# Fetching the first chunk of x as fp32 from two hardware queues, with the cast on VectorE and ScalarE

## The chip, the cores and the metric

The kernel runs on one core of a Trainium2 chip. A core has a matrix engine (TensorE, PE in the profile; its weight loads are listed apart as PEld), a vector engine (VectorE, DVE), an engine for activations (ScalarE, ACT), a general one (GpSimd, POOL) and one that only issues transfers (SyncE, SP). Sixteen DMA engines carry out the transfers of all queues. In the profile, q0 is the queue that GpSimd fills by software, q1 is SyncE's hardware queue and q10 is ScalarE's. The metric is the device time of one execution in microseconds; smaller is better.

## The reference

```python
def _attn_ref(x, filt_r, filt_i):
    X = np.fft.rfft(x, axis=1)
    F = (filt_r + 1j * filt_i)[None, :, :]
    Y = X * F
    y = np.fft.irfft(Y, n=x.shape[1], axis=1)
...
def _moe_ref(x, w_gate, w_val, w_out, rms_g):
    rms = np.sqrt(np.mean(x * x, axis=-1, keepdims=True) + 1e-06)
    xn = x / rms * rms_g
    g = xn @ w_gate
    silu = g * (1.0 / (1.0 + np.exp(-g)))
    val = xn @ w_val
    return (silu * val @ w_out).astype(np.float32)
```

x has 8 sequences of 3008 rows of 256 fp32 numbers. Each sequence is filtered along its length in the frequency domain, and each of the 24064 resulting rows then goes through a normalisation and a gated feed-forward layer of width 1536.

## The kernel before

The Fourier transforms are matrix products. 3008 is split as 64 times 47: the first step, a product with the 128x128 matrix `wa`, transforms along the 64; the second one, with `wb`, along the 47; the product with the filter and the way back (`wi`, `wai`) follow. Then every block of 512 rows is normalised and goes through the feed-forward products (lines 546 and 563), which fill nearly the whole span. While one sequence is in the feed-forward layer, the transforms of the next ones are fitted between its products by a planner (from line 718 on). Before that stands a prologue of about 44 us, written out by hand in program order, in which sequence 0 is transformed with nothing to overlap it. The change lies at the start of this prologue, and the steps of the prediction are all in it.

Each of the 128 partitions holds 24 rows of a sequence (the last of every other partition is not used), and x is loaded in four chunks of 6 of them (`XC = 6`, `NXC = 4`). `x_load` (line 174) takes a tile of pool `xp` in fp16 and has GpSimd's queue load and cast it in one transfer, since x lies in memory as fp32; GpSimd's queue is the one that casts. In the prologue GpSimd issues, in this order: the four chunks of sequence 0 (lines 614 and 615), the blocks of the filter `fs` (`f_load`, line 382), the tables `wb` and `wi`, and the weights. At most eight of its transfers are in flight: the ninth waits until the first has landed. SyncE issues the table `tab`, which holds `wa`, `wai` and the identity matrices (line 616), and three small loads of the last filter row and the norm's gain into `tail`.

TensorE starts with `fill(10)`: ten products of zeros with zeros (line 426) that compute nothing. `a0_unit` (line 353) then does the first step for four rows of each partition: four products of 128x128 with a slice of x as the stationary operand and `wa`, a part of `tab`, as the moving one (line 357), and a copy of the result (`psa`) to `uu`. `a0(g)` does both halves of group g, with ScalarE copying the one and VectorE the other (`copy`, line 193, whose own lines 195 and 197 stand in the profile). Group 0 needs rows 0 to 3 and group 1 rows 4 to 7, so that group 0 needs two thirds of chunk 0, and group 1 the rest of it and the start of chunk 1. The order on TensorE is as follows; between the second and the third row of fills stand five small transposes of `tail` (lines 650 and 651):

```python
        fill(10)
        a0(0)
        fill(4)
        a0(1, 2)
        ...
        fill(3)
        a0(3)
        fill(4)
        a0(4, 5)
```

After that come `f_unit` (line 385), which transposes the filter blocks through TensorE into `psf` (line 389), and `tr0_unit` (line 367), which transposes the result of the first step; then the second step for sequence 0.

The pool `stg` has four buffers. They are used in turn by the filter blocks, the weights before their scaling (`w_load`) and, later, the rows before the norm (`y_tile`).

Of the kernel before, what the change touches and what calls it, by code (L numbers as in the profile page):

```python
# [10 lines left out]
FP32 = mybir.dt.float32  # L11
FP16 = mybir.dt.float16
# [5 lines left out]
N1 = 47  # L18
N2 = 64
NF = N // 2 + 1  # L20
P = 128
D = 256
# [3 lines left out]
H = 24  # L26
# [7 lines left out]
XC = 6  # L34
NXC = H // XC
# [66 lines left out]
def kernel(  # L102
# [11 lines left out]
    nc = tc.nc  # L114
# [9 lines left out]
    stg = ctx.enter_context(tc.tile_pool(name="stg", bufs=4))  # L124
    xp = ctx.enter_context(tc.tile_pool(name="xp", bufs=4))
# [38 lines left out]
    st = {b: {"x": {}, "t1": {}, "t2": {}, "s": {}, "yt": {}, "t4": {}, "y": {}, "sq": {},  # L164
              "u": {}, "xn": {}} for b in range(B)}

    def raw(src, row, ap):
        return bass.AP(tensor=src.tensor, offset=src.offset + row * D, ap=ap)
# [5 lines left out]
    def x_load(b, c):  # L174
        t = xp.tile([P, XC, D], FP16, tag="xc", name="xc")
        row = b * N + c * XC
        src = lambda n, w, lo=0: raw(x.flatten_outer_dims(), row + lo, [[N1 * D, n], [H * D, 2], [1, w * D]])
        if b == B - 1 and c == NXC - 1:
            w = XC - 1
            nc.vector.memset(t[96:P, w, :], 0.0)  # L180
            nc.gpsimd.dma_start(t[:, 0:w, :].rearrange("p a d -> p (a d)"), src(N2, w))
            nc.gpsimd.dma_start(t[0:P - 2, w, :], src(N2 - 1, 1, w))
            nc.gpsimd.dma_start(t[P - 2:P - 1, w, :],
                                raw(x.flatten_outer_dims(), row + w + (N2 - 1) * N1, [[D, 1], [1, D]]))
        else:
            nc.gpsimd.dma_start(t.rearrange("p a d -> p (a d)"), src(N2, XC))  # L186
        st[b]["x"][c] = t

    def bank(i, name):
        pool, tag = ((psM, "mx"), (psG, "pg"), (psV, "pv"), (psB, "mb"), (psO, "po0"))[i]  # L190
        return pool.tile([P, 512], FP32, tag=tag, name=name)

    def copy(eng, out, in_, scale=None):
        if eng == "A":
            nc.scalar.activation(out=out, in_=in_, func=AXT.Copy, **({} if scale is None else {"scale": scale}))  # L195
        elif scale is None:
            nc.vector.tensor_copy(out=out, in_=in_)
        else:
            nc.vector.tensor_scalar(out=out, in0=in_, scalar1=scale, scalar2=None, op0=ALU.mult)
# [223 lines left out]
    def fill(n, bk=0):  # L423
        ps = bank(bk, "pf")
        for _ in range(n):
            nc.tensor.matmul(ps, ss3[0][:, 0, 0, :], ss3[0].rearrange("p k e q -> p (k e q)")[:, 0:512], start=True, stop=True)
# [181 lines left out]
                                        op0=ALU.mult, op1=ALU.mult)  # L608

    with tc.manual_schedule():  # L610
        nc.vector.memset(ss3[0], 0.0)
        nc.vector.memset(epsb, 1e-6 * Y_SCALE * Y_SCALE)
        nc.scalar.activation(out=warm, in_=epsb.to_broadcast([P, 4]), func=AXT.Sqrt)
        for c in range(NXC):
            x_load(0, c)
        nc.sync.dma_start(tab, tab_d)
        tail = op.tile([P, 4, D], FP32, tag="o3", name="tail")
# [20 lines left out]
        def a0(*gqs):  # L638
            for gq in gqs:
                for dh in range(2):  # L640
                    a0_unit(gq, dh, E[dh], 1 + dh)

        fill(10)
        a0(0)
        fill(4)
        a0(1, 2)
# [32 lines left out]
        for p in range(UN + 3):  # L679
            if 3 <= p < UN:  # L680
                b_unit(0, od[p], (0, 3)[p % 2])
                s_part(0, od[p], 1)
            if p == 0:
                f_unit(2, 1, 1, "A")
                f_neg(4, 12, (1,))
                f_last()
                f_neg(0, 4)
                w_load(2)
                wo_load(0)
                f_neg(16, 16)  # L690
                wo_load(1)
                for c in range(3):
                    x_load(1, c)
                for q in range(3):
                    w_gain(q)
            if 2 <= p < UN + 1:
                yt0_unit(od[p - 2], "A", 1)
            if p == UN + 1:
                yt0_unit(UN - 1, "V", 1, slice(0, 2))
                yt0_unit(UN - 1, "A", 0, slice(2, 4))  # L700
            if 4 <= p < UN + 3:
                bi_unit(0, od[p - 4], "AV"[p == UN + 1], 2)
            if UN + 1 <= p < UN + 3:
                fill(1, 1)
# [8 lines left out]
        nc.gpsimd.tensor_copy(out=seen, in_=st[0]["t4"][1][:, 0, 0:4])  # L713
        wo_load(2)
        x_load(1, 3)
        first_norm()

# [92 lines left out]
        for b in range(1, B):  # L810
            t = (b - 1) * 72
# [73 lines left out]
```

## Time and profile before

| | |
|---|---|
| time, median of 3 runs | 863.4 us (863.33 to 864.85) |
| span of the profiled execution | 861.4 us |
| TensorE busy | 852.4 us, 99% of the span |
| ScalarE busy | 612.4 us, 71% |
| VectorE busy | 557.2 us, 65% |
| GpSimd busy | 297.8 us, 35% |
| read from HBM, written to it | 45.78 MB, 35.65 MB |

The profile is that of one execution. Its span begins with the first instruction that was recorded and ends with the last; times within it are counted from its start. A row of the timeline gives the start, the duration from the first to the last of the grouped instructions, the engine, the line, the operation, the tiles (written one, arrow, read ones), their shape and number, and in brackets how long the engine had been idle before and what ended that. SPq is SyncE's queue of issues; the duration of a DMA row there is that of issuing, not of the transfer. A row of the chain that ended last gives start, duration and what the end of the program was waiting on then. A row of a DMA queue gives its packets, the megabytes and the share of the sixteen engines' time in that window.

### The profile page before, as it was taken

Reading aid. Unit: us, or ns where it says so; the run is one execution under the profiler, and the core shown is the slowest. Engines: PE = TensorE matmul, PEld = TensorE weight load, DVE = VectorE, ACT = ScalarE, POOL = GpSimd, SP = SyncE. Lnnn points to the kernel's source line nnn. Section 1 sums busy time; section 2 is a strip of 40 time slices with the busy share of each in tenths; the row PEclk is TensorE's granted clock in tenths of the full one; section 3 lists DMA queues with packets and bytes.
Section 4 is the critical chain, followed back from the end, with each engine's and each line's share of the span. In section 5 each row is a group of like instructions: output and inputs, shape, how many; then the busy total and the mean of one; then the engine's idle time right before and its main releaser. Section 6 shows DMA issues by size and latency. Waiting matters only on the chain.

```text
span 861.4 us, 17024 instructions
## 1 busy us (share of the span) xinstructions
PE 852.4 (99%) x6142; PEld 532.2 (62%) x6142; DVE 557.2 (65%) x926; ACT 612.4 (71%) x1339; POOL 297.8 (35%) x346
## 2 busy tenths in 40 slices
PE   8999999999999999999999999999999999999997
PEld 6755666566666666666666666666666666665664
DVE  5857655776666666666666676767666665555554
ACT  4986777787588756887577856888567765777443
POOL 5725742453144322534034430444123430132000
PEclk9999999999999999999999999999999999999999
DMA  9995778765975476656755548433564331521101
GB/s 283 270 204 124 150 164 168 139 130 121 197 137 129 121 150 111 151 107 147 139 127 113 132 98 180 108 87 101 131 127 93 97 70 42 124 54 49 62 25 50
DMA packets 198237, 107.98 MB, mean 125 GB/s; under 512 B 158566, under 2 KB 182520, under 8 KB 198152
## 3 DMA queue, kind: packets, MB, share of 16 engines
q1 hardware_dynamic: 189464, 85.52, 44.1%
q0 software_dynamic: 8544, 21.24, 12.7%
q8 instruction: 48, 0.79, 0.4%
q14 instruction: 37, 0.30, 0.1%
q10 hardware_dynamic: 144, 0.13, 0.0%
HBM read 45.78 MB, written 35.65 MB: 95 GB/s over the span
## 4 chain that ended last, share of the span: by engine, by line
PE 96%; DMA 1%; ACT 1%; DVE 1%; issue 0%; POOL 0%; POOLq 0%
PE po L563 28%; PE pg L546 28%; PE pv L546 28%; PE psb L241 3%; PE psi L285 3%; PE psn L314 2%; PE psa L206 2%; DMA fs<-in_filt_i_dram 1%; PE psy L418 1%; PE psf L389 1%; PE pst L367 0%; ACT sg L550 0%; POOL xc L186 0%; DVE s L231 0%; DVE hh L551 0%
## 5 line engine op out<-in xcount | busy, mean ns | idle before, releaser
L551 DVE TENSOR_TENSOR hh<-pv,sg 128x512 f16<-128x512 f32 (+2 forms) x578 | 391.5, 678 | 286.4 <-ACT sg L550 221.9
L550 ACT ACTIVATE sg<-pg 128x512 f16<-128x512 f32 (+2 forms) x578 | 337.4, 584 | 217.6 <-PE pg L546 213.4
L546 PE MATMUL pg<-xn,wg 128*128 128x512 f16 (+2 forms) x1156 | 338.1, 374 | 0.1
L546 PE MATMUL pv<-xn,wv 128*128 128x512 f16 (+2 forms) x1156 | 338.1, 374 | 0.0
L563 PE MATMUL po<-wo,hh 128*128 128x256 f16 x2256 | 332.7, 273 | 0.0
L563 PEld LDWEIGHTS <-hh 128*128 128x128 f16 x2256 | 213.4, 98 | 105.5 <-issue 0.6
L268 POOL TENSOR_TENSOR ss<-s,s 128x384 f16<-128x384 f16 x112 | 101.9, 911 | 273.2 <-DVE s L234 245.2
L546 PEld LDWEIGHTS <-wv 128*128 128x128 f16 x1156 | 112.9, 98 | 130.7
L546 PEld LDWEIGHTS <-wg 128*128 128x128 f16 x1156 | 111.4, 98 | 17.0 <-issue 0.3
L340 POOL TENSOR_TENSOR xt<-y,rho 128x1024 f16<-128x1024 f32 (+1 forms) x46 | 85.4, 1856 | 2.8
L322 ACT ACTIVATE junk<-y 128x256 f16<-128x256 f32 x180 | 74.3, 413 | 2.8
L231 DVE TENSOR_TENSOR s<-psb,ff 128x384 f16<-128x384 f32 x124 | 67.6, 547 | 0.7 <-ACT ff L195 0.6
L234 DVE TENSOR_TENSOR s<-psb,ff 128x384 f16<-128x384 f32 x124 | 67.6, 546 | 0.0
L195 ACT ACTIVATE uu<-psi 128x384 f16<-128x384 f32 (+1 forms) x127 | 61.6, 486 | 1.5 <-DMA out_dram<-o 0.5
L195 ACT ACTIVATE y<-psn 128x512 f32<-128x512 f32 (+1 forms) x95 | 55.7, 588 | 4.2
L285 PEld LDWEIGHTS <-yt 96*128 96x128 f16 x512 | 35.4, 97 | 26.7 <-issue 1.0
L332 POOL TENSOR_TENSOR rho<-u,mhalf 128x4 f32<-128x4 f32 (+1 forms) x46 | 46.5, 1010 | 3.8
L330 POOL TENSOR_SCALAR u<-ss 128x4 f32<-128x4 f32 (+1 forms) x46 | 8.9, 193 | 104.8 <-ACT junk L322 103.8
L195 ACT ACTIVATE t<-psa 128x512 f16<-128x512 f32 x70 | 41.4, 594 | 3.1 <-PE psa L206 1.7
L285 PE MATMUL psi<-wi,yt 96*128 96x96 f16 x512 | 42.9, 205 | 0.1
L241 PE MATMUL psb<-wb,t 96*128 96x96 f16 x480 | 40.1, 206 | 0.3 <-DVE s L234 0.2
L241 PEld LDWEIGHTS <-t 96*128 96x128 f16 x480 | 28.7, 97 | 12.8 <-DVE s L234 3.3
(101 smaller groups left out, 366.2 us busy)
## 6 DMA issues: line engine op xcount, KB each, us to landing
out_dram<-o SPq DMA_DIRECT2D x40, 512.0 KB, 3.6
xc<-in_x_dram POOLq DMA_DIRECT2D x31, 384.0 KB, 5.6
z_tmp<-t SPq DMA_DIRECT2D x28, 384.0 KB, 2.7
t<-z_tmp SPq DMA_DIRECT2D x28, 384.0 KB, 6.0
out_dram<-o SPq DMA_DIRECT2D x7, 384.0 KB, 2.7
fs<-in_filt_i_dram POOLq DMA_DIRECT2D x3, 512.0 KB, 10.8
fs<-in_filt_r_dram POOLq DMA_DIRECT2D x3, 512.0 KB, 11.2
ws<-in_moe_w_gate_dram POOLq DMA_DIRECT2D x3, 512.0 KB, 9.8
```

The source lines that it names most:

```text
L195: nc.scalar.activation(out=out, in_=in_, func=AXT.Copy, **({} if scale is None else {"scale": scale}))
L231: eng.tensor_tensor(out=o, in0=ps, in1=f1, op=ALU.mult)
L234: eng.tensor_tensor(out=o, in0=ps[:, :, ::-1, :], in1=f2, op=ALU.mult)
L241: nc.tensor.matmul(ps[:, ts(k, KR)], st[b]["t2"][kk // KC][:, kk % KC, ds(dh * P, P)], wb[0:KR, kk, :], start=True, stop=True)
L268: nc.gpsimd.tensor_tensor(out=ss3[g % 3][:, :, dh, 0:KR], in0=s[0], in1=s[1], op=ALU.add)
L285: nc.tensor.matmul(ps[:, k, :], yt[0:KR, k, dh, :], wi[0:KR, 4 * g + k, :], start=True, stop=True)
L322: nc.scalar.activation(out=junk, in_=y[:, i, ts(u, D)], func=AXT.Square, accum_out=ss[:, 2 * i + u:2 * i + u + 1])
L340: nc.gpsimd.tensor_tensor(out=xt[:, 0:n, :], in0=y.rearrange("p a (u d) -> p (a u) d", u=2)[:, 0:n, :], in1=rho[:, 0:n].unsqueeze(2).to_br ...
L546: nc.tensor.matmul(ps[:, 0:w], wt[:, dt_, ts(jt, P)], xn[:, q0:q1, dt_, :], start=(dt_ == 0), stop=(dt_ == 1))
L550: nc.scalar.activation(out=sg[:, c], in_=pg[:, 0:w], func=AXT.Silu)
L551: nc.vector.tensor_tensor(out=hh[:, c], in0=pv[:, 0:w], in1=sg[:, c], op=ALU.mult)
L563: nc.tensor.matmul(po[s4 // 2][:, s4 % 2, :], hh[:, ts(s4, P)], wo[:, jt, :], start=(jt == 0 and s4 % 2 == 0), stop=(jt == JT - 1 and (s4 ...
```

## The change

The first chunk of sequence 0 is no longer loaded by GpSimd. A new function `x_first` takes its fp16 tile as before and a staging buffer in fp32 from `stg`, and issues two transfers without a cast: SyncE loads the first four rows of each partition (`X0 = 4`), ScalarE the other two. It is called ahead of everything else, so that these are the first instructions of the two engines: `tab` and the three small loads come behind SyncE's part, and the load of ScalarE's function table comes behind ScalarE's part. GpSimd begins with chunk 1. On TensorE the first row of fills is cut from ten to seven. After it in program order VectorE casts the first four rows to fp16 and ScalarE the other two, ahead of their copies of `psa`.

```diff
+    X0 = 4
+
+    def x_first():
+        t = xp.tile([P, XC, D], FP16, tag="xc", name="xc")
+        raw_t = stg.tile([P, XC, D], FP32, tag="stg", name="xs")
+        for eng, lo, hi in ((nc.sync, 0, X0), (nc.scalar, X0, XC)):
+            eng.dma_start(raw_t[:, lo:hi, :].rearrange("p a d -> p (a d)"),
+                          raw(x.flatten_outer_dims(), lo, [[N1 * D, N2], [H * D, 2], [1, (hi - lo) * D]]))
+        st[0]["x"][0] = t
+        return t, raw_t
...
     with tc.manual_schedule():
+        xt0, xs0 = x_first()
         nc.vector.memset(ss3[0], 0.0)
         nc.vector.memset(epsb, 1e-6 * Y_SCALE * Y_SCALE)
         nc.scalar.activation(out=warm, in_=epsb.to_broadcast([P, 4]), func=AXT.Sqrt)
-        for c in range(NXC):
+        for c in range(1, NXC):
             x_load(0, c)
         nc.sync.dma_start(tab, tab_d)
...
-        fill(10)
+        fill(7)
+        copy("V", xt0[:, 0:X0, :], xs0[:, 0:X0, :])
+        copy("A", xt0[:, X0:XC, :], xs0[:, X0:XC, :])
         a0(0)
```

## The prediction

> **What bounds the kernel now.** I read the chain that ended last first, for the whole span and then for its first 45 us.
>
> ```profile
> PE 96%; DMA 1%; ACT 1%; DVE 1%; issue 0%; POOL 0%; POOLq 0%
> ...
> 1.25 2.37 POOL xc L186 x4
> 3.63 9.27 DMA fs<-in_filt_i_dram
> 12.90 0.14 issue
> 13.03 1.06 PE psf L389 x8
> ```
>
> TensorE is the bound for 96% of the span; what is not TensorE lies mostly before 13.03 us, where the chain is GpSimd's issuing and one row of transfers in a queue. From 13.03 on the chain runs over TensorE, ScalarE and VectorE alone, so whatever moves the row at 13.03 moves the end by as much. The timeline of that stage:
>
> ```profile
> 0.73 0.36 SPq L616 DMA_DIRECT2D tab<-tab_t  x1
> 1.25 2.65 POOL L186 DMA_DIRECT2D xc<-in_x_dram  x4 [0.82 <-POOLq L869]
> 1.45 4.45 PE L426 MATMUL pf<-ss 128*128 128x512 f16 x10 [1.45 <-DVE epsb L612]
> 6.06 1.03 PE L357 MATMUL psa<-tab,xc 128*128 128x128 f16 x8 [0.17 <-DMA xc<-in_x_dram]
> 6.89 1.14 PE L426 MATMUL pf<-ss 128*128 128x512 f16 x4
> 7.86 1.06 PE L357 MATMUL psa<-tab,xc 128*128 128x128 f16 x16
> 8.16 0.54 POOL L623 DMA_DIRECT2D wb<-wb_t  x1 [1.32 <-DMA xc<-in_x_dram]
> 9.25 0.82 PE L426 MATMUL pf<-ss 128*128 128x512 f16 x3
> 10.07 0.53 POOL L382 DMA_DIRECT2D fs<-in_filt_r_dram  x1 [1.37 <-DMA xc<-in_x_dram]
> 11.68 0.96 PE L357 MATMUL psa<-tab,xc 128*128 128x128 f16 x14 [0.18 <-DMA xc<-in_x_dram]
> 11.91 0.54 POOL L625 DMA_DIRECT2D wb<-wb_t  x1 [1.31 <-DMA xc<-in_x_dram]
> 13.03 1.06 PE L389 MATMUL psf<-tab,fs 128*128 128x128 f32 x8 [0.40 <-DMA fs<-in_filt_i_dram]
> ```
>
> Two things are to be seen. The waits of GpSimd's issues end when chunks land: at 8.16, 10.07 and 11.91, so a chunk takes 1.87 us; the first filter block follows at about 12.9. And TensorE has two speeds: eight L357 matmuls take 1.03 us at 6.06, sixteen take 1.06 at 7.86. Taking off the last one's own latency (up to 0.32, then 0.22), one follows another after 0.107 us, then after 0.056. The L426 fills do the same: (4.45 - 0.64)/9 = 0.42 at first, (0.82 - 0.38)/2 = 0.22 later. The speed doubles in the fills that begin at 6.89, about 7.1, or 5.6 us after the first fill. (The granted-clock column shows 1.00 throughout and hides this.)
>
> How queues share the engines is seen later, where a GpSimd load of x and a SyncE store run together (packets by queue, 122.25 to 124.25 us), and what one queue moves alone (15 to 17 us):
>
> ```profile
> q0 software_dynamic: 88, 0.27, 69.0%
> q1 hardware_dynamic: 86, 0.26, 36.0%
> ```
>
> ```profile
> q0 software_dynamic: 224, 0.85, 103.5%
> ```
>
> With both waiting, the engines take one packet of each in turn (88 to 86). Alone, a queue moves 0.85 MB in 2 us, 424 GB/s.
>
> **The change, part by part.**
>
> *Loading.* A GpSimd load of 384 KB (768 KB read) goes, and two transfers of 512 and 256 KB in fp32 take its place: the bytes read are the same. They start sooner. SyncE's first transfer was issued at 0.73 and moved its first bytes at 1.7; GpSimd's was issued at 1.25 and moved them at 2.75. The old start leaves the engines idle or slow until about 3.6; the new one fills about 1.3 us of that, so I expect chunks 1 to 3 and the filter blocks 0.7 to 1.4 us earlier. GpSimd issues one transfer less (0.66 us by its row, 2.65/4), and the eight transfers it may have in flight reach one further; it was far ahead, so this is worth nothing by itself, and the waits at 8.16, 10.07 and 11.91 move with the landings.
>
> *What is moved behind it.* On SyncE, tab (the DFT matrix and the identities) and three small tail loads now stand behind 512 KB of x. Every L357 matmul reads tab. Per engine, SyncE's x is 8 packets of 4 KB (512 KB at 424 GB/s is 1.24 us, 0.155 each), ScalarE's 8 of 2 KB (0.62, 0.078 each), tab 8 of 1.25 KB (it moved between 1.7 and 2.6; at 424 GB/s 0.39, with overhead 0.058 each), an x chunk of GpSimd's 8 (1.87/8 = 0.234 each). From 1.72 to 2.75 the two new transfers have the engines to themselves; less 0.2 for slow first packets that is 0.83 us, 3.5 of 8 rounds of 0.234. From 2.75 each round also holds a GpSimd packet: 4.5 x 0.468 = 2.1, so SyncE's x is in at 4.85. Then tab, packet for packet with GpSimd's queue, which is never empty: 8 x (0.058 + 0.234) = 2.34, in at 7.2. GpSimd's first packets are slow in the trace before (20 packets from 2.7 to 3.6, against 112 per us later); that adds 0 to 0.6 here, and I take 0.3. From last packet to first matmul took about 0.35 (a chunk lands at about 5.7, the matmul starts at 6.06). TensorE's first L357 matmul then starts at 7.5 + 0.35 = 7.85, between 7.55 and 8.15, against 6.06 before.
>
> The Trainium skill, DMA: Bandwidth & Descriptors, section Queues, rings and completion order, says that an engine drains a whole packet of typically 9 to 17 descriptors from one ring before it switches. By that tab's 8 would go in one turn; the count of 88 to 86 speaks for one each. What it would give is rival B.
>
> *The casts.* VectorE copies 128x1024 fp32 to fp16, a form the trace lacks. Its CAST of 128x512 took 0.69, so between 0.69 (two elements in the time of one) and 1.38; I take 1.0. From 4.85 + 0.3 + 0.35 = 5.5 it ends at 6.5, behind tab: hidden, and bare only if tab comes early. ScalarE's 128x512 is the 0.60 of its psa copies and is needed only by the second group. Behind both waiting casts stand only the copies of psa, which need TensorE anyway (they waited 4.3 and 4.5 us before). ScalarE's DMA issue delays its table load by some 0.4; ScalarE idles until 6.71. The tail loads land behind tab, before their matmuls of 8.85 move to about 12. The staging buffer that xs takes is next wanted by a weight load behind far later landings: nothing.
>
> *The fills and the clock.* Three fills go: 7 x 0.424 end at 4.4, not 5.7. TensorE then idles 3.4 us until 7.85, and starts slow. From there to the last L357 matmul it has 48 of these, 11 fills and five small transposes: 48 x 0.056 + 11 x 0.217 + 0.40 = 5.48 us at the fast speed, and each slow microsecond adds half. How long is it slow? At least 0, if it has kept the fast speed, at most the 5.6 of the first rise. I take 4.8, near the upper end, because the idle stretch is longer than the seven fills (3.0): +2.4. The last matmul is reached at 7.85 + 5.48 + 2.4 = 15.73. By then chunks 1 to 3 and the filter block have landed, and L389 can follow at once instead of at 13.03: +2.7 us. All later work is compute chained to this, so nothing wins it back.
>
> The Trainium skill, TensorE: Matmul & The Clock Gate, section The HAM clock gate, names about 3.4 us of sustained work in a free-running window for the rise, and a fall after an idle window. The 5.6 of this trace is longer; by 3.4 the slow part would cost 1.7, and the sum would be +2.0.
>
> *Sum.* The profiled execution spans 861.4; the median of the runs is 863.4, 2.0 more, and I add the change to that: 866.1. The own range of this case: a start between 7.5 and 8.2 with 3 to 5.6 us slow, +1.4 to +3.5, so 864.8 to 866.9.
>
> **The rivals.**
>
> *B, tab is not held up.* Its eight packets go in one turn, or the new transfers are served first. Then x is in at 3.2 to 4, tab at 4.7 to 5.3, the cast ends by 5.7: TensorE starts near 5.4. It is still slow, since the fills end at 4.4 and leave a gap: 5.4 + 5.48 + 2.4 = 13.28 against 13.03, +0.25: 863.6 (863.0 to 864.1). Against it stands the count of packets.
>
> *C, faster: the landings decide.* TensorE starts by 5.4 and its speed rises at 7.1 as before; then it waits for chunks. All transfers up to chunk 3 are 2.3 + 3 x 1.87 = 7.9 us of engine time from 1.9, so it lands at 9.9 to 10.5, the filter block 1.25 later, and L389 starts at 11.5 to 12.1: 1.2 us sooner, 862.2. The waits in the trace speak for it (each of chunks 2 and 3 is waited for); the shortened fills and the place of tab against it. It decides from a start before 5.05 (slow for 4.8) or 7.0 (fast from 7.1) on. Its bound is a whole chunk, 1.87.
>
> *D, tab late, but the fast speed kept.* 7.85 + 5.48 = 13.33: +0.3, 863.7. It needs a rise within the 3.0 us of seven fills, which before took 5.6.
>
> **How the numbers follow.** The forecast has 0.62, B 0.15, C 0.14, D 0.09. 0.2% is 1.7 us, about what a measurement of this kernel can tell from no change. The forecast exceeds it in nine parts of ten: slower 0.57. C exceeds it only near its bound: faster 0.05. The rest, 0.38, is within. The range runs from 862.9, which leaves out most of C, to 867.2, a little over the forecast's own.
>
> **What would show it.** In the changed profile: the first L357 matmuls near 7.85, waiting for tab and not for the cast; 0.107 between them; packets of tab spread over some 2 us; GpSimd's chunk waits ending 0.7 to 1.4 sooner; no wait for x or filters behind it; L389 near 15.7. A first L357 before 6, or L389 before 13, would prove the forecast wrong.

## The result and the profile after

The changed kernel takes 866.95 us (median of 5 runs, 864.46 to 867.94) against 863.33 for the kernel before: a ratio of 1.0036, with a 95% interval of 1.0024 to 1.0048. That is 3.6 us, where 2.7 were forecast. The profiled execution spans 865.2 us, 3.8 more than that of before. The lines of the changed kernel lie 11 to 12 further down: L368 is the old L357 (first step), L437 the fills, L400 the filter's transposes into `psf`, L635 the transfer whose wait ends when chunk 1 lands.

The chain that ended last, for the whole span and then for the first 17 us (start, duration, what the end was waiting on):

```profile
PE 96%; ACT 1%; DVE 1%; DMA 1%; issue 0%; SPq 0%
...
0.73 0.68 SPq L195
1.41 0.06 issue
1.47 7.28 DMA tab<-tab_t
8.75 0.04 issue
8.79 1.01 PE psa L368 x8
9.80 1.71 PE pf L437 x4
11.51 1.39 PE psa L368 x16
```

Before, the chain began with GpSimd's issues and ended its stretch of transfers with a filter block at 13.03. Now one transfer of SyncE, `tab`, is nearly the whole head of the chain: issued at 1.47, and waited for until 8.75. From there on no other wait of TensorE in the span is put down to a load. The timeline of the same stretch:

```profile
1.45 3.17 PE L437 MATMUL pf<-ss 128*128 128x512 f16 x7 [1.45 <-DVE epsb L624]
5.32 0.69 DVE L208 CAST xc<-xs 128x1024 f16<-128x1024 f32 x1 [2.50 <-DMA xs<-in_x_dram]
8.12 0.54 POOL L635 DMA_DIRECT2D wb<-wb_t  x1 [1.99 <-DMA xc<-in_x_dram]
8.79 1.01 PE L368 MATMUL psa<-tab,xc 128*128 128x128 f16 x8 [4.17 <-DMA tab<-tab_t]
13.88 0.61 PE L368 MATMUL psa<-tab,xc 128*128 128x128 f16 x8
16.27 1.14 PE L400 MATMUL psf<-tab,fs 128*128 128x128 f32 x8
```

Four things are to be seen. The first L368 had waited 4.17 us, for `tab`; the cast had been done since 6.01. Eight such matmuls take 1.01 us there and 0.61 at 13.88: after its idle stretch TensorE was as slow as in its first fills (seven in 3.17 us), which end at 4.62, before the speed had risen. The wait for chunk 1 ends at 8.12, as it did before (8.16), so nothing of x came sooner. And L400 starts at 16.27 instead of 13.03: 3.24 us late. The last store is issued at 860.97 instead of 857.64, 3.33 late; so nothing was won back, and 0.47 us more were lost behind the last store.

The queues between 5.7 and 8.2 us (packets, megabytes, share of the sixteen engines' time) show what held `tab` up:

```profile
q0 software_dynamic: 153, 0.42, 85.6%
q1 hardware_dynamic: 141, 0.16, 21.9%
```

127 of the 141 packets on SyncE's queue are `tab`, of 1.25 KB (its first one began at 5.69), the rest small. Between them the engines carried GpSimd's 153, of which 137 are pieces of x of 3 KB. The counts alone would also fit bursts of several packets; the times of the packets do not: 119 times a 3 KB packet begins 3 to 4 ns before a packet of `tab` ends, and 18 times another packet of `tab` does, which is about what chance gives. So the two queues took turns, one packet each. In the kernel before, `tab` was the first transfer of all and moved between 1.72 and 2.59.

### The profile page after: what moved, and what is told of

It reads as the page before. It is cut to its first block, busy times and chain, and to the rows that moved or that the text cites. A ratio compares the mean times of both kernels' runs of the same rounds, so it can differ in the third digit from the quotient of the medians.

```text
span 865.2 us, 17023 instructions
## 1 busy us (share of the span) xinstructions
PE 852.2 (99%) x6139; PEld 532.5 (62%) x6139; DVE 558.4 (65%) x927; ACT 613.4 (71%) x1340; POOL 297.8 (34%) x345
## 4 chain that ended last, share of the span: by engine, by line
PE 96%; ACT 1%; DVE 1%; DMA 1%; issue 0%; SPq 0%
PE po L574 28%; PE pg L557 28%; PE pv L557 28%; PE psb L252 3%; PE psi L296 2%; PE psn L325 2%; PE psa L217 2%; DMA tab<-tab_t 1%; PE psy L429 1%; PE psf L400 1%; PE pf L437 0%; PE psa L368 0%; PE pst L378 0%; DVE hh L562 0%; ACT sg L561 0%; DVE s L242 0%
```

## The experiments

All kernels compute the whole reference. Diffs are against the changed kernel unless another is named. Times are medians; before was 863.24, 863.24 and 863.31 in the three groups of runs (first e1 to e4, then e5 to e8, then e9 to e12). A summary first, with the start of `psf` (L389 before), the start of the last store, and the time from there to the end of the span, each from the one profiled execution, which need not be a typical one (that of e3 is its fastest):

| kernel | time, us | ratio to before, 95% | psf | last store | store to end |
|---|---|---|---|---|---|
| before | 863.33 | | 13.03 | 857.64 | 3.76 |
| changed | 866.95 | 1.0024 to 1.0048 | 16.27 | 860.97 | 4.23 |
| e1 | 868.44 | 1.0046 to 1.0071 | 17.98 | 862.70 | 4.20 |
| e2 | 865.06 | 1.0008 to 1.0025 | 14.50 | 859.21 | 4.19 |
| e3 | 868.75 | 1.0045 to 1.0071 | 14.62 | 859.33 | 4.17 |
| e4 | 863.39 | 0.9993 to 1.0010 | 12.98 | 857.64 | 3.76 |
| e5 | 864.11 | 1.0002 to 1.0020 | 13.99 | 858.69 | 4.21 |
| e6 | 864.39 | 1.0006 to 1.0024 | 13.33 | 858.33 | 4.17 |
| e7 | 869.26 (one run) | | 18.56 | 863.28 | 4.22 |
| e8 | 864.39 | 1.0004 to 1.0022 | 14.15 | 858.80 | 3.70 |
| e9 | 864.26 | 1.0002 to 1.0020 | 14.00 | 858.65 | 3.65 |
| e10 | 864.38 | 1.0004 to 1.0022 | 12.80 | 857.78 | 4.22 |
| e11 | 863.30 | 0.9992 to 1.0011 | 13.18 | 857.85 | 3.75 |
| e12 | 863.80 | 0.9997 to 1.0015 | 13.04 | 857.73 | 4.17 |

### Is it the place of tab? (e1, e3)

```diff
+        nc.sync.dma_start(tab, tab_d)
         xt0, xs0 = x_first()
...
-        nc.sync.dma_start(tab, tab_d)
```

e1 is that alone, so that SyncE issues `tab` and then its part of x; e3 has `fill(11)` for `fill(7)` as well.

> The changed kernel with one line moved: SyncE issues tab ahead of its part of x. My theory (tab late, then a slow TensorE): tab lands near 3, SyncE's x near 5.4, the cast of 0.69 ends near 6.2, so the first L368 matmul starts at 6.0 to 6.7 and no longer waits for tab. TensorE is still slow for 3.1 to 5.6 us after the gap, so the first psf matmul comes at 13.4 to 14.6 instead of 16.27, and the time at 863.7 to 865.0. Rival, the fp32 load and the cast themselves cost: still above 866. Rival, once tab is there the earlier landings win: 862.3 or less.

> Both at once: tab first and 11 fills. Theory: the first L368 matmul near 6.3, fast from about 7.1 on, then held by the landing of chunk 3 near 11.6 as in the kernel before, the first psf matmul at 12.7 to 13.3: 863.0 to 863.7, the same as before. If chunk 3 lands sooner than in the kernel before, as I had forecast for the changed kernel, 862.2.

Both missed: 868.44 and 868.75, worse than the changed kernel. `tab` was in at 2.6, but the delay had only changed its victim. From the timeline of e1:

```profile
9.41 0.69 DVE L208 CAST xc<-xs 128x1024 f16<-128x1024 f32 x1 [6.59 <-DMA xs<-in_x_dram]
9.87 0.55 POOL L635 DMA_DIRECT2D wb<-wb_t  x1 [3.90 <-DMA xc<-in_x_dram]
10.16 1.03 PE L368 MATMUL psa<-tab,xc 128*128 128x128 f16 x8 [5.64 <-DVE xc L208]
```

VectorE waited until 9.41 for x. SyncE's x, now its second transfer, moved from 3.00 to 8.83 in the trace; as its first transfer it had needed 3.09 to 4.95. GpSimd's queue had begun at 3.38, so x shared the engines with it from then on, and its last five packets moved after 7.5. The chunk that it shared with came late in turn (9.87). So it isn't `tab` that is harmed, but whatever stands second on SyncE's queue. (The profiled execution of e3 took 865.28 us: the cast starts at 8.12 and the first matmul at 8.87, at the fast speed. Its other five took 867.76 to 869.52 and have no profile, so what they lost is open.)

### Is GpSimd's queue what stretches the second transfer? (e7)

```diff
         xt0, xs0 = x_first()
...
+        nc.sync.dma_start(tab, tab_d)
+        nc.gpsimd.tensor_copy(out=seen, in_=tab[:, 0:4])
         for c in range(1, NXC):
             x_load(0, c)
-        nc.sync.dma_start(tab, tab_d)
```

GpSimd now reads a few columns of `tab` before its first load, so that its queue stays empty until `tab` is in.

> The changed kernel in which GpSimd does a tiny copy of four columns of tab before its first load, so that its queue stays empty until tab has landed. If GpSimd's packets are what stretches tab over 2.5 us, tab lands within 1 us of the end of SyncE's x, at 5.5 to 6.3, and the first L368 matmul starts at 6.1 to 6.8 instead of 8.8. The chunks then land some 2 to 2.5 us later, and the time is 865 to 868. If tab is late for another reason, the first matmul stays near 8.8.

From the timeline of e7:

```profile
5.94 0.33 POOL L627 COPY seen<-tab 128x4 f16<-128x4 f16 x1 [5.50 <-DMA tab<-tab_t]
6.28 0.62 PE L368 MATMUL psa<-tab,xc 128*128 128x128 f16 x8 [1.81 <-DVE xc L208]
11.20 1.67 PE L368 MATMUL psa<-tab,xc 128*128 128x128 f16 x14 [3.32 <-DMA xc<-in_x_dram]
11.44 0.55 POOL L636 DMA_DIRECT2D wb<-wb_t  x1 [0.51 <-DMA xc<-in_x_dram]
```

The order of transfers on SyncE is that of the changed kernel, yet `tab`'s packets now take 0.99 us (4.56 to 5.55) instead of 2.50 (5.69 to 8.19), and the first matmul starts at 6.28 instead of 8.79. That shows GpSimd's queue as the cause, both of the later begin (1.13) and of the longer stretch (1.51). The chunks pay for it: the first comes 3.3 us later (11.44 instead of 8.12), where 2 to 2.5 were expected. The time of the single run, 869.26, is 1.3 above the expected 865 to 868, but not by the chunks alone. TensorE waited 3.32 us for the first of them and lost its speed: 14 matmuls take 1.67 us at 11.20, against 0.95 in e4 at 7.88, and the profile's granted clock, which the prediction found at 1.00 throughout in the kernel before, is 0.50 here from 13 to 17 us. How the excess divides between the two was not separated.

### How much is TensorE's slow start? (e2, e4)

e2 has `fill(17)` for `fill(7)` in the changed kernel, so that TensorE is at work until `tab` lands. e4 is the kernel before with `fill(7)` for `fill(10)`.

> The changed kernel with 17 fills instead of 7, so that TensorE works from 1.45 until near the landing of tab. Theory: the first L368 matmul still starts near 8.8, but the spacing is 0.056 from the first one on, so the first psf matmul comes near 14.5 instead of 16.27: 865.0 to 865.6, with a smaller spread than the 3.5 us of the changed kernel's runs if the slow stretch is what varies. Rival, the place of tab is all and the speed after the gap costs nothing: 866.9 as before, or more if the fills end after tab lands.

> The kernel before with only the first row of fills cut from 10 to 7. Theory: the first matmul on x starts at 6.06 as before but TensorE stays slow for 3.1 to 5.6 us after it instead of 1.0; a part of this lies in the waits for chunks 2 and 3 (0.75 us in all). The first psf matmul comes at 13.3 to 14.4: 863.6 to 864.8. Rival, the fills are only padding: 863.3.

One row from e2 and one from e4:

```profile
8.77 0.61 PE L368 MATMUL psa<-tab,xc 128*128 128x128 f16 x8 [0.69 <-DMA tab<-tab_t]
```

```profile
6.02 0.62 PE L357 MATMUL psa<-tab,xc 128*128 128x128 f16 x8 [1.40 <-DMA xc<-in_x_dram]
```

e2 hit: `tab` still lands where it did, the matmuls are at the fast speed at once, and `psf` is at 14.50 instead of 16.27. So 1.77 us of the loss are the slow start, and the medians agree (866.95 - 865.06 = 1.89), as far as runs of the changed kernel that spread over 3.5 us can. e4 missed, and its rival was right: with three fills fewer in the kernel before nothing changes (863.39). After an idle stretch of 1.40 us the matmuls run at the fast speed at once, although the seven fills had run at the slow one; after 4.17 us in the changed kernel they were slow, and e7 shows a loss outright, from fast matmuls until 7.88 to slow ones at 11.20. Three fills fewer thus cost nothing by themselves. Whether ten would have been enough with the late `tab` was not run; e2 has seventeen.

### Can x be loaded so without a late second transfer? (e5, e6, e8, e9)

All four issue `tab` first on SyncE and have `fill(10)`. They differ in who loads the six rows of chunk 0:

| | rows 0 to 3 | rows 4 and 5 |
|---|---|---|
| e5 | ScalarE, fp32 | SyncE (second, behind `tab`), fp32 |
| e6 | ScalarE, fp32 | ScalarE (second), fp32 |
| e8 | GpSimd, cast in the transfer | ScalarE, fp32 |
| e9 | ScalarE, fp32 | GpSimd, cast in the transfer |

```diff
-        for eng, lo, hi in ((nc.sync, 0, X0), (nc.scalar, X0, XC)):
+        for eng, lo, hi in ((nc.scalar, 0, X0), (nc.sync, X0, XC)):
```

That is e5's; in e6 both parts name `nc.scalar`; in e8 and e9 one part is left in the list, and a `nc.gpsimd.dma_start` of the other, into the fp16 tile, stands behind it, and its cast on VectorE or ScalarE goes.

> The changed kernel with the order of the transfers mended: SyncE issues tab first and then the smaller part of x (rows 4 and 5), ScalarE the larger part (rows 0 to 3), and the ten fills are back. Theory, formed after the first four runs: on each hardware queue the first transfer moves before GpSimd's queue has begun, and the second one shares the engines with GpSimd's packets and is late, whichever it is. Then tab is in near 2.6, rows 0 to 3 near 4.2, the first L368 matmul starts at 5.2 to 5.9; rows 4 and 5 are late, but chunk 3 and the filter block land as in the kernel before, since as many bytes move, and the first psf matmul comes near 13.0: 863.0 to 863.9. Rival, loading in fp32 and casting costs in itself: 864.5 or more. Rival, the earlier start is worth something: 862.3 or less.

> As the run with the larger part on ScalarE's queue, but with both parts of x on ScalarE's queue, rows 0 to 3 first, and tab alone ahead on SyncE's. Theory: the same, 863.0 to 863.9; rows 4 and 5 are the second transfer of a queue and land after 6, packet for packet with GpSimd's.

> A version that keeps what may be of use: tab first on SyncE, GpSimd loads and casts rows 0 to 3 of chunk 0 and then the other chunks, and only rows 4 and 5 go in fp32 through ScalarE's queue, into the time in which GpSimd's first packets are slow; ten fills. Theory: 256 KB leave GpSimd's queue, at 424 GB/s up to 0.6 us, so that chunk 3 lands 0 to 0.6 sooner than in the kernel before: 862.6 to 863.4. Rival, ScalarE's transfer delays the start of GpSimd's by as much: 863.3 or a little more.

> tab is SyncE's first transfer, rows 0 to 3 of chunk 0 are ScalarE's first one (fp32, cast on VectorE), rows 4 and 5 are GpSimd's first one (cast in the transfer), so that no queue has to begin a second transfer before the matmuls. If a second transfer on a hardware queue was what came late: cast of rows 0 to 3 by 5.5 us, first matmul by 6.2, second group of matmuls not held up (rows 4 and 5 in by 6), chunk landings at 8.2, 10.1 and 11.9 as before since the bytes are the same, psf at 13.0 to 13.4; 863.4 to 863.9, of which 0 to 0.7 at the program's end. Rival, the engines start earlier and the chunks land 0.7 sooner: 862.6 or less. Rival, GpSimd's first packets crawl beside the other two, as when GpSimd loaded rows 0 to 3: landings 1 us later and 864.4 or more.

They measured 864.11, 864.39, 864.39 and 864.26: 0.9 to 1.2 us over before, none in its expected range. But TensorE now starts at 5.66 to 6.24, so the 2.7 us at its start are gone. What is left is of another kind. In e5 and e6 the second transfer is late again: rows 4 and 5 are cast at 8.84 and 8.19, and the second group of matmuls waits. In e8 and e9 no hardware queue has a second transfer of x, and the landings are late instead. From the timeline of e9 (two lines further down than in the changed kernel):

```profile
5.66 0.61 PE L370 MATMUL psa<-tab,xc 128*128 128x128 f16 x8
9.18 0.54 POOL L637 DMA_DIRECT2D wb<-wb_t  x1 [2.50 <-DMA xc<-in_x_dram]
14.00 1.07 PE L402 MATMUL psf<-tab,fs 128*128 128x128 f32 x8 [0.45 <-ACT uu L208]
```

The wait for chunk 1 ends at 9.18, 1.0 us later than before (8.16), and `psf` and the last store follow by 1.0. In the trace of e9 the first packet of GpSimd's queue moves at 3.86, against 2.75 before, although GpSimd issued at 1.25 in both; until 4.47 ScalarE's 512 KB hold the engines. In e8, e1, e10 and the changed kernel that first packet moves at 3.08, 3.38, 3.93 and 4.55. So a fp32 load in front does not only use idle time: with it GpSimd's queue begins 0.3 to 1.8 us later. That this begin is what makes the chunks late in e8 and e9 was only argued. In e8 it comes 0.33 later and the wait for chunk 1 ends 1.1 later (9.27); in e10, where GpSimd has no part of chunk 0 to load first, it comes 1.18 later and that wait ends at 7.85, earlier than before.

### Landings, or TensorE's own path? (e10)

e6, with nine fills in the wait for rows 4 and 5, and those of the later places (4, 3 and 4) left out:

```diff
-        fill(4)
+        fill(9)
         a0(1, 2)
...
-        fill(3)
         a0(3)
-        fill(4)
         a0(4, 5)
```

> As the version with both parts on ScalarE, but the fills that stood after the first matmuls, the transposes and the fourth group (4, 3 and 4) are nine in the wait for rows 4 and 5. If its 0.3 us at psf came from TensorE's own work after 8.87 us: psf at 13.0 to 13.1, waiting for the filter block, and 0.2 to 0.3 less than that version's 864.4. If it came from the landings (which were those of before): psf at 13.3 and 864.4 again. Of the rest, 0.7 is expected at the program's end either way.

`psf` started at 12.80, 0.5 us ahead of e6 and 0.23 ahead of the kernel before, and yet the median was 864.38, no better than e6. GpSimd's wait for the first filter block ended 0.23 earlier than before as well (12.95 against 13.18). So part of what e6 lacked was TensorE's own path: in e6 `psf` starts 0.07 behind the end of GpSimd's wait for the filter block (13.26), in e10 0.15 ahead of it, as in the kernel before, which makes 0.22. The other 0.31 are the landings, which came earlier from chunk 1 on (7.85 against 8.26) although both kernels issue the same transfers; a start shorter than before has thus been seen in one execution only. The gain went at two places of the profiled execution, which spans 862.0. One is in the chain that ended last of e10, at 35 us, still in the prologue:

```profile
34.85 0.19 PE psi L296 x4
35.04 0.24 issue
35.28 0.59 ACT yt L206
35.87 0.38 ACT uu L206
```

ScalarE stood still for 0.35 us before a copy whose input was there; the chain puts the first part down to TensorE's `psi`, which ended at 35.04, and calls the other 0.24 "issue", waiting for nothing that the profile shows. e6 has the same stop at the same copy (35.84, also 0.35), and no other kernel here has it. These two are the ones in which ScalarE issues both parts of x, so its stream of instructions is one longer than in the changed kernel; what makes it stop was not tried, and stays open. After it TensorE is 0.10 behind the kernel before, instead of 0.23 ahead. The other place is the end of the program, +0.46 (next). The profiled execution thus accounts for 0.6 of the 1.07 us of the median; the rest lies in executions that have no profile here.

### What is lost behind the last store? (e11, e12)

Both are the kernel before with nothing of the change, only with more and smaller transfers on hardware queues: the small load of a last filter row in two halves, for one of the two rows (e11), or for both, with one half issued by ScalarE (e12, whose edit is shown).

```diff
-            nc.sync.dma_start(tail[0:1, f, :], raw(src, NF - 1, [[D, 1], [1, D]]))
+            nc.sync.dma_start(tail[0:1, f, 0:P], raw(src, NF - 1, [[D, 1], [1, D]])[:, 0:P])
+            (nc.sync, nc.scalar)[f].dma_start(tail[0:1, f, P:D], raw(src, NF - 1, [[D, 1], [1, D]])[:, P:D])
```

> The kernel before with one small load of the last filter row split in two halves, so one more hardware transfer and nothing else. Theory: the number of hardware transfers shifts the order in which SyncE passes its closing waits; then the work up to the last store is where it was (psf at 13.0, last store issued at 857.6) and the time from there to the end differs by 0.1 to 0.8 us: 863.4 to 864.1 against 863.2 of before. Rival: the end of the program doesn't depend on it, 863.2 within 0.1.

> The kernel before with both small loads of the last filter row split in two, one of the halves issued by ScalarE: one more hardware transfer on SyncE and one on ScalarE, as in the changed kernel, and nothing else. Theory: psf at 13.0 and the last store issued at 857.6 as before, and 0.5 to 0.8 us more from there to the end, as in the changed kernel: 863.7 to 864.1. Rival: no dependence, 863.2 within 0.1, and the 0.5 of the changed kernel's end have another cause.

The first row of the following answers is the span, the second SyncE's last store. Before, then e12:

```profile
core 0 of [0], span 861.4 us
857.64 0.56 SPq L578 DMA_DIRECT2D out_dram<-o  x1
```

```profile
core 0 of [0], span 861.9 us
857.73 0.54 SPq L578 DMA_DIRECT2D out_dram<-o  x1
```

From the last store to the end it is 3.76 us before and 4.17 in e12; e11 has 3.75. One transfer more changes nothing, so e11 went by its rival, and two cost 0.4, a little under the 0.5 to 0.8 of e12's theory. The last column of the table says the same of all kernels: those with no or one more hardware transfer (before, e4, e8, e9, e11) have 3.65 to 3.76, those with two more (all the others) 4.17 to 4.23, whatever else they do. The times bear it out less sharply: e12 is at 863.80, +0.49 of before, but its interval, 0.9997 to 1.0015, includes no difference. So in the profiles the loss of 0.4 to 0.5 at the end goes with the number of transfers. In the traces SyncE passes its closing waits in another order there; that this order is the mechanism was only argued.

## Why the prediction was right, and where its terms were off

The prediction named the mechanism and the sign, and the time lies within its range, 0.25 us from the upper end, though 0.05 beyond the 864.8 to 866.9 that it gave for its own case. That it came so near is in part luck: the start came 0.94 later than forecast and the slow stretch cost 0.65 less, which offset each other. Its terms compare with the runs as follows.

**tab stands behind x and shares with GpSimd's queue: right, mis-sized by 0.94.** The first matmul was forecast at 7.85 and came at 8.79, beyond the upper bound of 8.15. The stretch was right: 2.34 forecast, 2.50 measured, and e7 shows the cause by taking GpSimd's queue away. Wrong was when things begin. The forecast let SyncE's x move from 1.72, as `tab` had in the trace before, and share with GpSimd from 2.75; x really moved from 3.09, and until 4.55 without GpSimd's queue, so that the two errors cancelled (in at 4.95 against 4.85). Then GpSimd's queue began, at 4.55 and without the slow first packets for which 0.3 had been added (55 packets in its first 0.9 us, against 20 in the kernel before): `tab` began at 5.69 where 5.15 was implied (+0.54), its stretch added 0.16, and 0.60 instead of 0.35 lay between its last packet and the matmul (+0.25).

**The slow start of TensorE: right, mis-sized by -0.65.** It was put at 2.4. By e2 against the changed kernel it is 1.77, of which 0.02 are an earlier first matmul. The speed rose 3.6 us after the restart, not 4.8: the matmuls follow one another after 0.107 us up to 12.26 and after 0.056 from 12.45 on. By the Trainium skill, TensorE: Matmul & The Clock Gate, section The HAM clock gate, with some 3.4 us, the term would have been an estimated 1.7. The 1.75 measured here agree with it. But 4.8 was no worse a choice in general: after its restart TensorE stayed slow for 4.4 us in e1 (from 10.16) and for 6.6 in e7 (from 11.20). The size of this term thus changes from one kernel to another, and which one this kernel got is luck.

**The work from the first matmul to psf at the fast speed: 5.48, measured 5.73** (e2: 14.50 - 8.77), +0.25. These three terms give 0.94 + 0.25 - 0.65 = 0.54, the difference between 16.27 and the forecast 15.73.

**Chunks and filter blocks 0.7 to 1.4 us sooner: wrong.** The waits ended at 8.12, 10.14 and 11.96, against 8.16, 10.07 and 11.91. The step that failed is that the fp32 transfers fill time in which the engines were idle or slow. They begin at 2.17, no earlier than `tab` did before (1.72), and GpSimd's queue begins later: at 4.55 instead of 2.75. Counted over the packets until 8 us (GpSimd's twice, since they are fp16 behind the cast), the engines had read 2.15 MB instead of 2.07. It cost the sum nothing: with TensorE starting at 8.79 and slowly, no later group had to wait for its chunk.

**The casts hidden: right.** VectorE's cast took 0.69, the lower bound of its range (1.0 was taken), and ended at 6.01, 2.2 us before the last packet of `tab`.

**Nothing wins it back: right, but something was added.** The shift of 3.24 at `psf` is 3.33 at the last store. The 0.4 to 0.5 behind that store was no term of the sum; e12 shows it for two more transfers alone.

Of the rivals, B (tab in one turn) falls with the turns of one packet each and with e7. That was also what the Trainium skill, DMA: Bandwidth & Descriptors, section Queues, rings and completion order, would have given; this trace, with 127 packets of `tab` to 137 of x, does not bear it out. D (fast speed kept) falls with the 1.01 us of the first eight matmuls; it is, in effect, what e2 makes by hand. C (faster, by the landings) had the right idea of what would decide: e5, e6 and e8 to e10 remove the late start, and then the landings, a late second transfer or TensorE's own work set `psf`. But the best of them gained 0.23 us at `psf`, not 1.2, and none ends ahead of the kernel before.

## What to carry to other kernels

A queue that is served quickly by itself is slow as soon as another one is never empty: what stands second on it shares the engines packet for packet, and small packets lose against large ones (2.50 us for `tab` beside GpSimd's queue, 0.99 without it). Before a transfer is put in front of others, ask what becomes second, who waits for that, and when the other queue's first packet will move then. If the first operand of a matrix engine becomes late, the price has two parts, the wait and the slow speed after it; fills that reach to the landing took the second part away here (e2), and one run with more fills measures it.

## What the runs showed of the hardware that was not expected

A first transfer did not begin at a fixed time after its issue: SyncE's x, issued at 0.73, moved its first packet 2.36 us later, while `tab`, issued at the same time in the kernel before, took 0.99.

The moment at which TensorE's speed rises is not tied to the first matmul. e11 and the kernel before begin with the same instructions on TensorE, and their first eight matmuls take 0.62 us at 6.21 in the one and 1.03 at 6.06 in the other; e10 has 0.62 at 5.74. Nor is the slow stretch after a restart of one length: 3.6 us in the changed kernel, 4.4 in e1, 6.6 in e7.

The end of a program changed with the number of its transfers: two more small loads at its start, and 0.4 us more behind its last store, 858 us later.
